# Attention, rotary mixing and a gated MLP in one kernel: first loads reordered, staging tiles borrowed, three mixing items and one weight conversion moved later

## The chip, the cores and the metric

One Trainium2 chip, of which the kernel uses one core. The metric is the device time of one execution in microseconds (us); lower is better. The kernel before takes 564.57 us, the median of 3 runs (564.46 to 564.57).

## The reference

Three blocks follow one another on 4 batches of 576 positions and 512 channels. The first is attention with 8 heads of 64 channels: heads 0 to 3 look at the last 32 positions, heads 4 to 7 at every fourth of the last 128. The second computes an angle and mixes:

```python
theta = x @ w_theta
zr, zi = x * cos(theta), x * sin(theta)
y = einsum('ts,bsd->btd', w_tok_r, zr) + einsum('ts,bsd->btd', w_tok_i, zi)
u = x + y
x = u + maximum(u @ w_ch, 0)
```

The third is a gated MLP:

```python
h = maximum(x @ w_in, 0);  u, v = h[..., :512], h[..., 512:]
v_s = einsum('ts,bsd->btd', w_spatial, layernorm(v)) + b_spatial
out = (u * v_s) @ w_out
```

The weights `w_theta`, `w_tok`, `w_ch`, `w_in` and `w_out` come as 64-bit floats.

## The kernel before, in words

All large products run on PE as three float32r products (high by high, low by high, high by low), so every weight and every activation is split into a high and a low part. A 64-bit weight chunk goes through `bits64` (L115): a DMA into a `w64` tile (4 buffers), one scaling on POOL or ACT into a `stage` tile (4 buffers), three bit operations on DVE through one PSUM tile `c64`; then `split_weight` (L136) makes the high part (`copy`, L107 to L111) and the low part (a subtraction, L144). Weights of the third block go back to DRAM by `stored` (L152): both parts in a `parts` tile (2 buffers), then a DMA into `win_d`, `wsp_d` or `wo_d`, from where they are loaded when there is room.

The order of the program, batch by batch:

- `attention(b)` (L300) makes 12 groups (4 head pairs by 3): scores on PE (L240; for batch 0 the mask is added on PE too, L233), softmax on DVE, ACT and POOL (L247 to L258), transposes (L268) two groups later, products with V (L282, L286) four groups later; ACT copies the result into `x` (L289 to L298). `att_load` (L196) issues the loads of K, Q and V, all on the SP queue; for batch 0 it is called for all four head pairs at once.
- `th_unit` (L326) makes the angle of 128 positions: `x` split on ACT or DVE (L339 to L342), 12 matmuls (L347), four transposes of `x` (L359), sine and cosine on ACT (L364, L365), and z split into `zh`, `zl` tiles. The last 64 positions of batches 2 and 3 share one unit, `th_shared` (L388), which starts from a copy `xs` (L332).
- `tm_run` (L402) mixes over positions: 8 items per batch, each 3 matmuls for each of 9 chunks of positions (L418, L425). For batch 2 the 8 items are made over 8 chunks first (24 matmuls each), and the ninth chunk, which waits for the shared unit, later.
- `ch_run` (L433) makes the product with `w_ch` (L444), 8 steps, and stores the result to `x2d`.
- The third block, for each batch: `hv_unit` (L617, five units, the fifth shared by two batches) with the normalisation on DVE, `hu_run` (L661), `sp_run` (L679), `out_unit` (L708).

`spread` (L458) interleaves one generator with others at given rates, so that attention of the next batch and weight conversions stand between mixing items. `second` (L490) is the list of conversions for the third block: 16 of `w_in`, 8 of `w_sp`, 8 of `w_out`. Twelve are taken in batch 1's stage, ten in batch 2's first stage (L520), and the rest while batch 3's angles are made (L521).

The program order is a priority, not the final order: when the kernel is built (L814, `schedule_with_timeline_sim=True`) a scheduler simulates the engines and gives each engine a fixed list, taking what it believes ready first. On the chip each engine then works its list in order, and a late input holds all that stands behind it. `tc.issue_after(ins)` forces what is traced inside it on the engine of `ins` behind `ins` in that list; it adds no wait.

PSUM has eight banks: `ps_mm` 4 (scores, angles, mixing, `w_ch`), `ps_t` 3 (transposes, V products), `ps_v` 1 (`c64`). After the second block the last two give way to `ps_2` with 4, which the third block uses alone.

```python
spread(tm_run(PAIR, K_MAIN, False), (chain(attention(PAIR + 1), th_shared(PAIR)), ATT_RATE_PAIR), (take(second, 10), 1.25))
spread(th_run(PAIR + 1, (0, 1, 2, 3)), (chain(tm_run(PAIR, (8,)), ch_run(PAIR)), TAIL_RATE), (second, 2.5))
```

Of the kernel before, what the change touches and what calls it, by code (L numbers as in the profile page):

```python
# [62 lines left out]
def tile_block(ctx: ExitStack, tc: tile.TileContext, qT, kT, vw, eye_in, mask_in, eye_b_in, w_theta, w_tok, w_ch, w_in, w_sp, w_sph, b_sp, w_out, out):  # L63
# [32 lines left out]
    wth_h = pth.tile([P, 4, DM], F32R, name="wth_h")  # L96
    wth_l = pth.tile([P, 4, DM], F32R, name="wth_l")
    patt = tc.alloc_tile_pool(name="patt", bufs=2, side="right")
    ps_t = tc.alloc_tile_pool(name="ps_t", bufs=3, space=PSUM)

    ps_v = tc.alloc_tile_pool(name="ps_v", bufs=1, space=PSUM)
    c64 = ps_v.tile([P, 512], F32, name="c64")


    def copy(dst, src, eng):
# [6 lines left out]

    last_dma = [None]

    def bits64(src, n, eng):  # L115

        p = src.shape[0]
        st = const.tile([P, 2 * CH], U32, tag="w64", name="w64", bufs=4)  # L120
        last_dma[0] = SY.dma_start(st[:p, :2 * n], src.bitcast(U32))
        w = st[:p, :2 * n].rearrange("p (n w) -> p n w", w=2)
        lw, hw = w[:, :, 0], w[:, :, 1]
        g = const.tile([P, CH], F32, tag="stage", name="w64g", bufs=4)[:p, :n]
        c = c64[:p, :n].bitcast(U32)
        gi = g.bitcast(U32)
        if eng == "a":
            A.mul(g, hw.bitcast(F32), 2.0**-112)
        else:
            G.tensor_scalar(g, hw.bitcast(F32), 2.0**-56, 2.0**-56, op0=ALU.mult, op1=ALU.mult)  # L130
        V.tensor_scalar(c, lw, 29, None, op0=ALU.logical_shift_right)
        V.scalar_tensor_tensor(c, gi, 3, c, op0=ALU.logical_shift_left, op1=ALU.bitwise_or)
        V.scalar_tensor_tensor(gi, gi, 0x80000000, c, op0=ALU.bitwise_and, op1=ALU.bitwise_or)
        return g

    def split_weight(src, hi, lo, eng_hi, eng_lo, eng_bits="g"):  # L136
        n = hi.shape[-1]
        if src.dtype == F32:
            s = const.tile([P, CH], F32, tag="stage", name="stage", bufs=4)[:src.shape[0], :n]
            SY.dma_start(s, src)  # L140
        else:
            s = bits64(src, n, eng_bits)
        copy(hi, s, eng_hi)
        (G if eng_lo == "g" else V).tensor_tensor(lo, s, f32(hi), op=ALU.subtract)  # L144

# [12 lines left out]

    def w_theta_job(k, c):
        cs = slice(DM // 2 * c, DM // 2 * (c + 1))  # L160
        split_weight(w_theta[:, k, cs], wth_h[:, k, cs], wth_l[:, k, cs], *THETA_ENG)

    def w_tok_job(k, c):
        cs = slice(CH * c, CH * (c + 1))
# [27 lines left out]
    groups = [(b, hp, g) for b in range(B) for hp in range(4) for g in range(3)]  # L192
    att = {}
    heads = {}

    def att_load(b, hp):  # L196
        early = b == 0 and hp >= 2
        qz = qz_2[hp - 2] if early else qzero[hp % 2]
        kt = kt_2[:, hp - 2] if early else patt.tile([P, S + WIN], F32, tag="k", name="kt", bufs=2)
        first = b == 0 and hp == 0  # L200
        n = KW + (NA - 1) * T
        for c0, c1 in ((0, n), (n, S + WIN)) if first else ((0, S + WIN),):
            SY.dma_start(kt[:, c0:c1], kT[b, hp, :, c0:c1])
            if c0 == 0:
                SY.dma_start(qz[:D, 0], qT[b, hp, :D])
            if first and c0 == 0:
                SY.dma_start(masks[:, :1], mask_in[:, :1])
                SY.dma_start(eye_b, eye_b_in)
        SY.dma_start(qz[D:, 1], qT[b, hp, D:])
        if first:  # L210
            SY.dma_start(masks[:, 1:], mask_in[:, 1:])
            SY.dma_start(ident, eye_in)
        vt = vt_2[:KW, hp - 2] if early else patt.tile([KW, NT, P], F32, tag="v", name="vt", bufs=2)
        SY.dma_start(vt, vw[b, hp])
        heads[b, hp] = (qz, kt, vt, {})
# [56 lines left out]
    def att_values(m):  # L272

        b, hp, g = groups[m]
        if g == 0:
            return
        qz, kt, vt, pT = heads[b, hp]
        ps = ps_t.tile([P, 512], F32, tag="pt", name="ps_x")
        if g == 1:
            for t in range(NA):  # L280
                for j in range(2):
                    PE.matmul(ps[T * j:T * (j + 1), T * t:T * (t + 1)], vt[:, t, T * j:T * (j + 1)], pT[j][:, T * t:T * (t + 1)], start=True, stop=True)  # L282
        else:
            for t in range(NB):
                for j in range(2):
                    PE.matmul(ps[T * j:T * (j + 1), T * t:T * (t + 1)], vt[:, NA + t, T * j:T * (j + 1)], pT[2][:, P * t + T * j:P * t + T * (j + 1)], start=True, stop=True)  # L286
        n0, n1 = (0, NA * T) if g == 1 else (NA * T, S)
        if hp < 2:
            A.copy(x[b][:, hp, n0:n1], ps[:, :n1 - n0])  # L289
            return  # L290

        xv = x[b][:, hp, :].rearrange("p (i r) -> p r i", r=4)
        if g == 1:
            A.copy(xv[:, :2, :], ps[:, :2 * SEQ].rearrange("p (r i) -> p r i", r=2))
            A.copy(xv[:, 2, :NA * T - 2 * SEQ], ps[:, 2 * SEQ:NA * T])
# [30 lines left out]
    def th_unit(b, t, pair=False):  # L326
# [29 lines left out]
        V.scalar_tensor_tensor(ta, ta, MAGIC, ps, op0=ALU.subtract, op1=ALU.subtract)  # L356
        xn = ps_t.tile([P, 512], F32, tag="pt", name="ps_xn")[:n]
        for k in range(4):
            PE.transpose(xn[:, P * k:P * (k + 1)], src[:, k, :], ident)  # L359
        if b == 0:  # L360
            A.activation(tb, ta, AF.Abs)
        else:
# [225 lines left out]

    for _ in ch_run(3):
        w3()  # L590
    p1.release()

    p2 = tc.alloc_tile_pool(name="p2", bufs=1, side="left", reuse_waits="tile")
    ps_2 = tc.alloc_tile_pool(name="ps_2", bufs=4, space=PSUM)

    wo_h = p2.tile([P, 4, DM], F32R, name="wo_h")
    wo_l = p2.tile([P, 4, DM], F32R, name="wo_l")
# [1 line left out]
        SY.dma_start(f32(t), f32(wo_d[:, :, i]))  # L599

    def mmtile(name):
        return ps_2.tile([P, 512], F32, tag="m2", name=name)

    vh, vl, vhl = {}, {}, {}
    hu = {}
# [126 lines left out]
    for pr in (0, 2):  # L732
# [85 lines left out]
```

## Time and profile before

| | us |
|---|---|
| median of 3 runs | 564.57 |
| the profiled execution | 564.04 |
| its span, first to last instruction | 562.2 |
| PE busy | 535.4 (95%) |
| DVE busy | 323.7 (58%) |
| POOL busy | 261.7 (47%) |
| ACT busy | 245.6 (44%) |

PE, DVE, ACT and POOL are the matrix, vector, scalar and GpSimd engines, SP issues DMAs (SPq is its queue), PEld is PE's weight load. "PEclk" is the granted clock of PE as a share of 2.4 GHz; 0.5 is 1.2 GHz. In a timeline row the bracket gives the idle time ahead of the instruction and what ended it. Busy is the union of an engine's instructions in a stretch. The durations of matmuls overlap, so their spacing, not their sum, is their cost.

### The profile page before, as it was taken

The page shows a single profiled execution, that of the slowest core. Times are in us where ns is not written, and L with a number is a line of the kernel's source. Part 1 is how long each engine was busy: PE and PEld are TensorE (multiplying, and loading weights), DVE is VectorE, ACT ScalarE, POOL GpSimd, SP SyncE. Part 2 cuts the span into 40 slices and gives each one's busy share as a digit, 9 for nine tenths or more (in the row PEclk, how much of TensorE's full clock was granted, in tenths as well). Part 3 has the DMA queues.
Part 4 walks back from the last instruction along what each step waited for, and adds up shares of the span by engine and source line. Part 5 has one row for each costly group of instructions (what it writes and reads, how often), then busy time and mean ns, then how long its engine had stood idle before and what let it go on. Part 6 is the DMA issues. An engine that isn't in the chain of part 4 may idle for free.

```text
span 562.2 us, 11265 instructions
## 1 busy us (share of the span) xinstructions
PE 535.4 (95%) x4148; PEld 477.2 (85%) x4148; DVE 323.7 (58%) x834; ACT 245.6 (44%) x718; POOL 261.7 (47%) x333
## 2 busy tenths in 40 slices
PE   4987999999999999996999999999999999999997
PEld 2765878888888988885979999899899889988996
DVE  2588998898887378656697116763701237353030
ACT  3768855525656444776354112432331224223222
POOL 3483995545975259744269334344201204322040
PEclk9899999999999999998899999999999999999999
DMA  7944956561468352785301999614015110002002
GB/s 188 234 139 126 238 152 194 178 188 62 144 200 236 109 180 96 239 244 170 116 1 43 325 362 355 208 35 136 11 64 168 39 56 1 1 1 76 1 0 94
DMA packets 50079, 76.07 MB, mean 135 GB/s; under 512 B 4068, under 2 KB 30824, under 8 KB 50024
## 3 DMA queue, kind: packets, MB, share of 16 engines
q1 hardware_dynamic: 50024, 75.35, 44.0%
q8 instruction: 33, 0.54, 0.4%
q14 instruction: 22, 0.18, 0.1%
HBM read 52.53 MB, written 22.81 MB: 134 GB/s over the span
## 4 chain that ended last, share of the span: by engine, by line
PE 63%; DVE 11%; DMA 8%; POOL 6%; ACT 5%; issue 5%; SPq 1%; POOLq 0%; DVEq 0%; ACTq 0%
PE ps_y L425 12%; PE ps_sp L693 9%; PE ps_hu L674 9%; PE ps_o L722 9%; PE ps_hv L629 9%; PE ps_r L444 5%; PE s L240 3%; DMA wsp_d<-parts 2%; PE pt L268 2%; DMA win_d<-parts 2%; POOL zl L319 2%; PE ps_x L282 2%; POOL parts L144 1%; DMA qz<-qT 1%; DMA x2d<-parts 1%
## 5 line engine op out<-in xcount | busy, mean ns | idle before, releaser
L425 PE MATMUL ps_y<-wtok_h,zh 128*128 128x288 f32 x270 | 82.7, 309 | 2.4 <-DVE sm L251 1.4
L425 PE MATMUL ps_y<-wtok_h,zl 128*128 128x288 f32 x270 | 81.3, 302 | 0.4 <-POOL zl L319 0.4
L425 PE MATMUL ps_y<-wtok_l,zh 128*128 128x288 f32 x270 | 80.3, 300 | 0.0
L319 POOL TENSOR_TENSOR gl<-hu,gh 128x288 fp32r<-128x288 f32 x32 | 26.0, 814 | 74.5 <-ACT gh L107 74.5
L425 PEld LDWEIGHTS ps_y<-wtok_h,zh 128*128 128x128 f32 x270 | 51.0, 190 | 5.9 <-DVE sm L251 2.1
L697 DVE TENSOR_TENSOR hu<-ps_sp,hu 128x288 f32<-128x288 f32 x32 | 14.6, 456 | 66.7 <-PE ps_sp L696 66.7
L425 PEld LDWEIGHTS ps_y<-wtok_h,zl 128*128 128x128 f32 x270 | 51.3, 190 | 1.9 <-POOL zl L319 0.8
L425 PEld LDWEIGHTS ps_y<-wtok_l,zh 128*128 128x128 f32 x270 | 51.0, 190 | 0.5
L319 POOL TENSOR_TENSOR vl<-hv,vh 128x512 fp32r<-128x512 f32 x16 | 20.9, 1308 | 62.6 <-ACT vh L107 55.2
L258 POOL TENSOR_TENSOR sm<-sm,l 128x288 f32<-128x288 f32 x48 | 32.6, 680 | 27.4 <-DVE l L257 22.1
L255 ACT ACTIVATE sm<-sm,m 128x96 f32<-128x96 f32 x108 | 39.2, 364 | 9.8 <-DVE m L252 7.5
L240 PE MATMUL s<-kt,qz 128*64 128x96 f32 x504 | 35.5, 268 | 4.6 <-DMA qz<-qT 3.4
L319 POOL TENSOR_TENSOR parts<-x,parts 128x288 fp32r<-128x288 f32 x32 | 26.6, 840 | 27.2 <-ACT parts L107 27.2
L693 PE MATMUL ps_sp<-wsp_h,vh 128*128 128x288 f32 x128 | 37.8, 295 | 0.0
L693 PE MATMUL ps_sp<-wsp_l,vh 128*128 128x288 f32 x128 | 37.8, 295 | 0.0
L693 PE MATMUL ps_sp<-wsp_h,vl 128*128 128x288 f32 x128 | 37.8, 295 | 0.0
L674 PE MATMUL ps_hu<-x2h,win_h 128*128 128x288 f32 x128 | 37.7, 294 | 0.0
L674 PE MATMUL ps_hu<-x2h,win_l 128*128 128x288 f32 x128 | 37.7, 294 | 0.0
L674 PE MATMUL ps_hu<-x2l,win_h 128*128 128x288 f32 x128 | 37.7, 294 | 0.0
L444 PE MATMUL ps_r<-uh,wch_l 128*128 128x288 f32 x128 | 37.7, 297 | 0.0
L444 PE MATMUL ps_r<-uh,wch_h 128*128 128x288 f32 x128 | 37.6, 298 | 0.0
L444 PE MATMUL ps_r<-ul,wch_h 128*128 128x288 f32 x128 | 37.4, 296 | 0.0
(180 smaller groups left out, 1570.0 us busy)
## 6 DMA issues: line engine op xcount, KB each, us to landing
x2d<-parts SPq DMA_DIRECT2D x32, 288.0 KB, 2.6
vt<-vw SPq DMA_DIRECT2D x16, 432.0 KB, 4.1
w<-w_tok SPq DMA_DIRECT2D x18, 288.0 KB, 3.0
x2h<-x2d SPq DMA_DIRECT2D x8, 576.0 KB, 7.4
x2l<-x2d SPq DMA_DIRECT2D x8, 576.0 KB, 10.7
kt<-kT SPq DMA_DIRECT2D x15, 304.0 KB, 5.3
w<-w_in SPq DMA_DIRECT2D x16, 256.0 KB, 3.5
win_d<-parts SPq DMA_DIRECT2D x16, 256.0 KB, 2.3
```

What stands on the lines that cost most here:

```text
L240: PE.matmul(o, qz[:, j, T * t:T * (t + 1)], kt[:, T * t:T * t + KW], start=not on_pe, stop=not on_pe)
L255: ia = A.activation(sm[:, t, :], src[:, t, :], AF.Exp, bias=m_[:, t:t + 1], scale=scale, accum_out=l[:, t:t + 1])
L258: ig = G.tensor_tensor(sm, sm, l.unsqueeze(2).to_broadcast([P, 3, KW]), op=ALU.mult)
L268: PE.transpose(pt[:KW, P * t:P * (t + 1)], sm[:, t, :], ident)
L319: return (G if el == "g" else V).tensor_tensor(dst_l, src, f32(dst_h), op=ALU.subtract)
L425: PE.matmul(ps[:, :CH], lh[b, k][:, P * d:P * (d + 1)], rh[:, k, cs], start=(n == 0), stop=(n == 3 * len(ks) - 1))
L444: PE.matmul(ps[:, :CH], lh[:, k, P * e:P * (e + 1)], rh[:, k, cs], start=(n == 0), stop=(n == 11))
L629: PE.matmul(ps, lh[:, k, ts_], rh[:, k, DM:], start=(n == 0), stop=(n == 11))
L674: PE.matmul(ps[:, :CH], lh[:, k, fs], rh[:, k, cs], start=(n == 0), stop=(n == 11))
L693: PE.matmul(ps[:, :CH], lh[b, k][:, fs], rh[:, k, cs], start=(n == 0), stop=False)
L697: V.tensor_tensor(t[:, f, cs], ps[:, :CH], t[:, f, cs], op=ALU.mult)
L722: PE.matmul(ps, lh[:, k, ts_], rh[:, k, cs], start=(n == 0), stop=(n == 11))
```

## The change

- `att_load`, batch 0: Q's first half and the small identity `eye_b` are issued from ACT's queue; the masks come in three pieces; V of a head pair is loaded one pair later, `ident` and the last masks with the second pair.
- `w_theta` is staged in the eight tiles `zh0..3`, `zl0..3`, which hold z later, and no longer in `w64`.
- Batch 2's mixing: five items are spread with attention of batch 3 and ten conversions; items six and seven are queued on PE behind the last V products of groups 46 and 47; then the shared unit and the first unit of batch 3; item eight is queued behind that unit's transposes.
- Two conversions (of `w_sp`) stay with batch 3's angles; the eight of `w_out` go, one per step, into `ch_run(3)`.
- `c64` is kept to the end; `ps_2` has 3 banks, and the third block alternates between `ps_2` and `ps_mm`.

```diff
-        split_weight(w_theta[:, k, cs], wth_h[:, k, cs], wth_l[:, k, cs], *THETA_ENG)
+        split_weight(w_theta[:, k, cs], wth_h[:, k, cs], wth_l[:, k, cs], *THETA_ENG, st=pz.tile([P, DM], U32, tag=f"z{'hl'[c]}{k}", name="wth64"))
...
-                SY.dma_start(qz[:D, 0], qT[b, hp, :D])
+                (A if first else SY).dma_start(qz[:D, 0], qT[b, hp, :D])
...
-                SY.dma_start(eye_b, eye_b_in)
+                A.dma_start(eye_b, eye_b_in)
...
-            SY.dma_start(masks[:, 1:], mask_in[:, 1:])
+            SY.dma_start(masks[:, 1:2], mask_in[:, 1:2])
...
+        if hp == 1:
             SY.dma_start(ident, eye_in)
+            SY.dma_start(masks[:, 2:], mask_in[:, 2:])
+        if hp:
+            SY.dma_start(heads[0, hp - 1][2], vw[0, hp - 1])
+        if hp == 3:
+            SY.dma_start(vt, vw[0, 3])
...
-    spread(tm_run(PAIR, K_MAIN, False), (chain(attention(PAIR + 1), th_shared(PAIR)), ATT_RATE_PAIR), (take(second, 10), 1.25))
-    spread(th_run(PAIR + 1, (0, 1, 2, 3)), (chain(tm_run(PAIR, (8,)), ch_run(PAIR)), TAIL_RATE), (second, 2.5))
+    tm = tm_run(PAIR, K_MAIN, False)
+    spread(take(tm, 7 - HELD), (attention(PAIR + 1), ATT_RATE_PAIR), (take(second, 10), 1.25))
+    for i in range(HELD):
+        with tc.issue_after(values[12 * (PAIR + 2) - HELD + i].ins):
+            next(tm)
+    run(th_shared(PAIR))
+    th = th_run(PAIR + 1, (0, 1, 2, 3))
+    next(th)
+
+    with tc.issue_after(turned[PAIR + 1, 0].ins):
+        run(tm)
+    spread(th, (chain(tm_run(PAIR, (8,)), ch_run(PAIR)), TAIL_RATE), (take(second, 2), 0.5))
...
     for _ in ch_run(3):
         w3()
+        next(second, None)
...
-    ps_2 = tc.alloc_tile_pool(name="ps_2", bufs=4, space=PSUM)
+    ps_2 = tc.alloc_tile_pool(name="ps_2", bufs=3, space=PSUM)
...
-        return ps_2.tile([P, 512], F32, tag="m2", name=name)
+        turn[0] += 1
+        return (ps_2 if turn[0] % 2 else ps_mm).tile([P, 512], F32, tag=("mm", "m2")[turn[0] % 2], name=name)
```

Here `HELD` is 2, `values[m]` is the last V product of group m and `turned[b, t]` the last transpose of a unit.

## Rows read from the trace of the kernel before

**Rows 1.** The page's busy time of PE, with share and number of instructions.
```profile
PE 535.4 (95%) x4148; PEld 477.2 (85%) x4148; DVE 323.7 (58%) x834; ACT 245.6 (44%) x718; POOL 261.7 (47%) x333
```
**Rows 2.** Busy time by stretch: start:end, length, then engines; granted clock, DMA share, GB/s.
```profile
4.75:13.00 8.25, 4.85 (x46) 3.02 (x46) 1.97 (x7) 3.73 (x21) 1.33 (x2) 0.91 0.95 224
24.70:45.00 20.30, 18.26 (x203) 12.89 (x199) 18.01 (x47) 13.77 (x53) 15.78 (x30) 1.00 0.51 145
45.00:84.30 39.30, 34.09 (x287) 28.55 (x287) 36.69 (x88) 31.61 (x85) 31.91 (x40) 1.00 0.64 174
84.30:224.00 139.70, 138.83 (x1234) 122.35 (x1233) 110.44 (x281) 70.58 (x215) 84.99 (x114) 1.00 0.54 160
224.00:258.40 34.40, 32.93 (x373) 28.54 (x371) 20.49 (x67) 24.27 (x99) 20.78 (x29) 1.00 0.73 222
258.40:265.30 6.90, 1.98 (x41) 1.54 (x40) 4.73 (x13) 4.53 (x15) 2.23 (x4) 0.91 0.63 188
265.30:272.30 7.00, 7.00 (x35) 6.90 (x36) 5.05 (x10) 1.69 (x5) 3.19 (x4) 0.60 0.54 171
272.30:295.50 23.20, 22.21 (x121) 18.77 (x119) 18.59 (x33) 11.29 (x20) 10.41 (x11) 1.00 0.10 30
343.00:376.50 33.50, 33.50 (x211) 31.00 (x210) 22.88 (x58) 13.38 (x32) 14.58 (x15) 1.00 0.51 174
```
**Rows 3.** PE's timeline at the start: start, us, instruction, idle before and its releaser.
```profile
4.75 0.42 PE L233 MATMUL s<-masks,eye_b 128*128 128x288 bf16 x1 [4.75 <-DMA eye_b<-eye_b]
...
12.98 1.23 PE L240 MATMUL s<-kt,qz 128*64 128x96 f32 x12 [3.40 <-DMA qz<-qT]
```
**Rows 4.** POOL's timeline: the first and the last operation on w_theta.
```profile
24.80 0.43 POOL L130 TENSOR_SCALAR w64g<-w 128x256 f32<-128x256 f32 x1 [0.47 <-DMA w<-w_theta]
...
42.07 0.73 POOL L144 TENSOR_TENSOR wth_l<-w64g,wth_h 128x256 fp32r<-128x256 f32 x1
```
**Rows 5.** SP's waits, 0 to 100 us: total, times, longest.
```profile
SPq L121 <- DVE c L131: 47.0, 24, 5.1
```
**Rows 6.** ACT's waits, 0 to 300 us: total, times, longest.
```profile
ACT parts L107 <- DMA wo_d<-parts: 6.4, 3, 3.5
...
ACT w64g L128 <- DMA w<-w_tok: 4.2, 3, 3.0
```
**Rows 7.** PE's timeline where attention of batch 3 ends.
```profile
259.25 0.50 PE L268 MATMUL pt<-ident,sm 128*96 128x128 f32 x3 [0.80 <-DVE pT L270]
...
261.92 0.57 PE L286 MATMUL ps_x<-pT,vt 96*64 96x64 f32 x12 [1.32 <-ACT pT L270]
265.29 1.09 PE L359 MATMUL ps_xn<-ident,xs 128*128 128x128 f32 x4 [2.80 <-DVE xs L332]
...
268.31 0.44 PE L425 MATMUL ps_y<-wtok_h,zh 128*128 128x288 f32 x1
```
**Rows 8.** ACT's and DVE's timeline in the same place.
```profile
263.34 0.40 ACT L107 CAST parts<-w64g 128x256 fp32r<-128x256 f32 x1 [0.53 <-DVE c L132]
263.65 0.66 ACT L294 COPY x<-ps_x 128x288 f32<-128x288 f32 x1
...
264.85 0.29 DVE L332 COPY xs<-x 128x256 f32<-128x256 f32 x1 [1.05 <-ACT x L298]
```
**Rows 9.** The chain that ended last, one mixing item of 27 matmuls.
```profile
108.11 3.60 PE ps_y L425 x27
```
**Rows 10.** DVE's timeline, first use of w_sp's last rows.
```profile
337.44 0.30 DVE L570 CAST wsp_hh<-stage 128x288 fp32r<-128x288 f32 x1
```
**Rows 11.** The shared normalised unit: DVE writes vhb, PE reads it.
```profile
375.63 0.42 DVE L658 CAST vhb<-hs 64x512 fp32r<-64x512 f32 x1
...
377.77 0.30 PE L696 MATMUL ps_sp<-wsp_lb,vhb 97*128 97x288 f32 x1
```
**Rows 12.** A DVE and a POOL operation side by side in the normalisation.
```profile
361.93 1.31 POOL L319 TENSOR_TENSOR vl<-hv,vh 128x512 fp32r<-128x512 f32 x1 [1.01 <-ACT vh L107]
362.19 1.07 DVE L642 TENSOR_TENSOR r<-r 128x1 f32<-128x1 f32 x1
```

More of the change, by code (lines that the diff above doesn't have):

```diff
@@ L49 @@
 PAIR = 2
+HELD = 2
 IN_ENG, SP_ENG, OUT_ENG = "vgg", "ag", "aga"
@@ L98, in tile_block @@
     patt = tc.alloc_tile_pool(name="patt", bufs=2, side="right")
-    ps_t = tc.alloc_tile_pool(name="ps_t", bufs=3, space=PSUM)
     ps_v = tc.alloc_tile_pool(name="ps_v", bufs=1, space=PSUM)
     c64 = ps_v.tile([P, 512], F32, name="c64")
+    ps_t = tc.alloc_tile_pool(name="ps_t", bufs=3, space=PSUM)
     def copy(dst, src, eng):
@@ L113, in tile_block, with bits64 @@
     last_dma = [None]
-    def bits64(src, n, eng):
+    def bits64(src, n, eng, st=None):
         p = src.shape[0]
-        st = const.tile([P, 2 * CH], U32, tag="w64", name="w64", bufs=4)
+        if st is None:
+            st = const.tile([P, 2 * CH], U32, tag="w64", name="w64", bufs=4)
         last_dma[0] = SY.dma_start(st[:p, :2 * n], src.bitcast(U32))
@@ L134, in bits64, with split_weight @@
         return g
-    def split_weight(src, hi, lo, eng_hi, eng_lo, eng_bits="g"):
+    def split_weight(src, hi, lo, eng_hi, eng_lo, eng_bits="g", st=None):
         n = hi.shape[-1]
@@ L141, in split_weight @@
         else:
-            s = bits64(src, n, eng_bits)
+            s = bits64(src, n, eng_bits, st)
         copy(hi, s, eng_hi)
@@ L194, in tile_block @@
     heads = {}
+    values = {}
     def att_load(b, hp):
@@ L204, in att_load @@
             if c0 == 0:
-                SY.dma_start(qz[:D, 0], qT[b, hp, :D])
+                (A if first else SY).dma_start(qz[:D, 0], qT[b, hp, :D])
             if first and c0 == 0:
                 SY.dma_start(masks[:, :1], mask_in[:, :1])
-                SY.dma_start(eye_b, eye_b_in)
+                A.dma_start(eye_b, eye_b_in)
         SY.dma_start(qz[D:, 1], qT[b, hp, D:])
         if first:
-            SY.dma_start(masks[:, 1:], mask_in[:, 1:])
-            SY.dma_start(ident, eye_in)
-        vt = vt_2[:KW, hp - 2] if early else patt.tile([KW, NT, P], F32, tag="v", name="vt", bufs=2)
-        SY.dma_start(vt, vw[b, hp])
-        heads[b, hp] = (qz, kt, vt, {})
+            SY.dma_start(masks[:, 1:2], mask_in[:, 1:2])
+        vt = vt_2[:KW, hp - 2] if early else patt.tile([KW, NT, P], F32, tag="v", name="vt", bufs=2)
+        heads[b, hp] = (qz, kt, vt, {})
+        if b:
+            SY.dma_start(vt, vw[b, hp])
+            return
+        if hp == 1:
+            SY.dma_start(ident, eye_in)
+            SY.dma_start(masks[:, 2:], mask_in[:, 2:])
[3 more added lines that the diff above has]
+            SY.dma_start(vt, vw[0, 3])
     def att_scores(m):
@@ L281, in att_values @@
                 for j in range(2):
-                    PE.matmul(ps[T * j:T * (j + 1), T * t:T * (t + 1)], vt[:, t, T * j:T * (j + 1)], pT[j][:, T * t:T * (t + 1)], start=True, stop=True)
+                    values[m] = PE.matmul(ps[T * j:T * (j + 1), T * t:T * (t + 1)], vt[:, t, T * j:T * (j + 1)], pT[j][:, T * t:T * (t + 1)], start=True, stop=True)
         else:
@@ L285, in att_values @@
                 for j in range(2):
-                    PE.matmul(ps[T * j:T * (j + 1), T * t:T * (t + 1)], vt[:, NA + t, T * j:T * (j + 1)], pT[2][:, P * t + T * j:P * t + T * (j + 1)], start=True, stop=True)
+                    values[m] = PE.matmul(ps[T * j:T * (j + 1), T * t:T * (t + 1)], vt[:, NA + t, T * j:T * (j + 1)], pT[2][:, P * t + T * j:P * t + T * (j + 1)], start=True, stop=True)
         n0, n1 = (0, NA * T) if g == 1 else (NA * T, S)
@@ L314, in tile_block @@
     zlast = {}
+    turned = {}
     uu = {}
@@ L358, in th_unit @@
         for k in range(4):
-            PE.transpose(xn[:, P * k:P * (k + 1)], src[:, k, :], ident)
+            turned[b, t] = PE.transpose(xn[:, P * k:P * (k + 1)], src[:, k, :], ident)
         if b == 0:
@@ L519, in tile_block @@
     th_keep(PAIR)
-    spread(tm_run(PAIR, K_MAIN, False), (chain(attention(PAIR + 1), th_shared(PAIR)), ATT_RATE_PAIR), (take(second, 10), 1.25))
-    spread(th_run(PAIR + 1, (0, 1, 2, 3)), (chain(tm_run(PAIR, (8,)), ch_run(PAIR)), TAIL_RATE), (second, 2.5))
+    tm = tm_run(PAIR, K_MAIN, False)
[9 more added lines that the diff above has]
+    spread(th, (chain(tm_run(PAIR, (8,)), ch_run(PAIR)), TAIL_RATE), (take(second, 2), 0.5))
     patt.release()
-    ps_v.release()
     ps_t.release()
@@ L590, in tile_block @@
         w3()
+        next(second, None)
     p1.release()
     p2 = tc.alloc_tile_pool(name="p2", bufs=1, side="left", reuse_waits="tile")
-    ps_2 = tc.alloc_tile_pool(name="ps_2", bufs=4, space=PSUM)
+    ps_2 = tc.alloc_tile_pool(name="ps_2", bufs=3, space=PSUM)
+    turn = [0]
     wo_h = p2.tile([P, 4, DM], F32R, name="wo_h")
@@ L755, in tile_block @@
     ps_2.release()
+    ps_v.release()
     p2.release()
```

## The prediction, made before the changed kernel ran

> **What bounds the kernel now.** I read the page's engine line first: PE is busy 535.4 of 562.2 us [rows 1], so 26.8 us without matmuls is nearly all there is to win, apart from the granted clock. The second view is the table of stretches, to see where those microseconds lie [rows 2]. From 84.3 to 224 us PE lacks 0.9 us of 139.7, and the stretch 343 to 376.5 has no gap: a faster side engine gives nothing there. The holes are in three places: the start (nothing until 4.75 us, then 3.40 of the next 8.25 us empty), the stage in which batch 0's angles are made (45 to 84.3 us: 5.2 us empty, with DVE busy 36.7 of 39.3), and the end of attention for batch 3 (258.4 to 265.3 us: 4.92 of 6.90 empty). Behind the last hole stands a second price: in the 7.00 us after it the granted clock is 0.60, that is mostly 1.2 GHz, with PE busy throughout; at 2.4 GHz that work would have taken 7.00 x 0.60 = 4.2 us, so 2.8 us are lost. The third view is the timeline at each hole, to see what ended it.
>
> **First loads.** Two waits stand at the start: the first matmul waits to 4.75 us for `eye_b`, and the first scores of head pair 1 wait 3.40 us for Q [rows 3]. All loads run in SP's order, and the DMA engines are 0.95 busy at 224 GB/s there [rows 2], so what counts is the bytes ahead. From the tile shapes (K 304 KB, Q 288, V 432, masks 4 x 72, `ident` 64, `eye_b` 32) pair 1's Q was behind 2000 KB and is now behind 1360: V of pair 0, `ident` and two masks moved back. 640 KB at 224 GB/s are 2.9 us, so the 3.40 us wait shrinks to some 0.5. `eye_b` goes from SP's fourth issue to ACT's second; I take 0.6 us (0 to 1.2; ACT has nothing else to do before the first scores are there). Attention of batch 0 is then 3.5 us ahead.
>
> Not all of that lives. Everything up to V of pair 3 is as many bytes as before, so the first chunk of `w_theta` can't come much before 24.80 us, when POOL starts on it; POOL ends the last at 42.07 + 0.73 = 42.8 [rows 4]. In those 18 us it does 8 chunks at 0.43 (L130) + as much for the high part, one input of the same size, + 0.73 = 1.6, so 12.7 us, and the softmax scalings still due, which are fewer by the lead. I let 2.5 of the 3.5 us live. Bounds: +1.0 (slower: V of pair 0 now lies behind 2000 KB instead of 1408, 592 KB or 2.7 us later, and the first V product may wait for it in PE's list) and -4.1 (2.9 + 1.2, all of it alive).
>
> **Staging `w_theta` in the z tiles.** SP waits 47.0 us in the first 100 for DVE to free a `w64` buffer, 24 times [rows 5]. With eight own tiles, `w_theta`'s loads wait for nothing, and four loads of `w_tok` can be under way before DVE reads any; ACT's waits for `w_tok`, 4.2 us in 3 [rows 6], go. What is late next is DVE: 36.7 of 39.3 us busy from 45 to 84.3 [rows 2], so no more than 2.6 us can be won there, and 2.3 (20.30 - 18.01) from 24.7 to 45. I take 1.5 us (0 to 4.9). The z tiles are first written after the chunks in them were read, since z needs the angle and the angle all of `w_theta`: no new wait.
>
> **Three items held back.** Before, two items of 24 matmuls stood behind the shared unit's transposes in PE's list and ran at 268.31, after the hole and mostly at the low clock, though they could have run in it [rows 7]. An item of 27 costs 3.60 us [rows 9], one of 24 then 3.2. Now one stands before the last V product (it covers the 1.32 us) and one behind it (it covers the 2.80 us from that product to `xs`); the 0.80 us ahead of them stays. The third stands behind the first unit's transposes and covers the split of `x`. So 4.1 us of holes go, and I let the clock's 2.8 us go with them, since PE then never rests there.
>
> The price is on the other side: one item that ran before 258.4 us is missing there. PE was busy 32.9 of 34.4 us in that stage, ACT 24.3, DVE 20.5 [rows 2]. If attention's chain follows PE, the stage ends 3.2 us sooner; if it goes at its own pace, 3.2 us become holes. I take 1.4. Sum for this part: -(4.1 + 2.8) + 1.4 = -5.5, between -10 (every hole from 224 to 295.5 us, 1.5 + 4.9 + 1.0, and the clock) and -0.9 (4.1 won, the 3.2 us come back whole and the clock stays).
>
> **`w_out` put off.** It is taken from the same place: the copy of `x` at 263.65 stands on ACT behind a cast for `w_out` that waited for DVE, and `xs` behind that copy [rows 8]; ACT waited 6.4 us there for `wo_d`'s stores [rows 6]. With the held items that chain is covered anyway, so I count it in the 1.4 above. Its new place is `ch_run(3)`. It needs `stage` tiles, and the four are with the last rows of `w_sp`, first read at 337.44 us [rows 10], so I expect it beside the first normalisations: 8 chunks of 1.3 us on DVE (three operations of this size at 0.43, as POOL's in [rows 4]), 0.8 on ACT (two at 0.40 [rows 8]), 0.73 on POOL. From 343 to 376.5 us these have 10.6, 20.1 and 18.9 us free [rows 2], but the normalisation's last write ends at 376.05, 1.7 us before PE needs it at 377.77 [rows 11]. I take 0 (0 to +12, worked out below). The parts themselves are wanted by `out_unit` alone, behind `hu_run`, `sp_run` and four units of the next batch.
>
> **PSUM.** Seven banks instead of four for the third block, in which PE had no gap: 0. `c64`'s longer life costs a bank that nothing wanted.
>
> **Sum.** -2.5 - 1.5 - 5.5 = -9.5. The profiled execution took 564.04 us (1.84 around the span), so 554.5; the median is 0.53 above that execution, so **555.1 us**.
>
> **Rivals.**
>
> *The hole only moves.* Attention of batch 3 keeps its own pace, the missing item leaves 3.2 us open, and the clock falls all the same. For it: DVE, ACT and POOL wait on one another there, none is full. Against it: PE was 96% busy. Then -2.5 - 1.5 - 4.1 + 3.2 = -4.9: 559.7 us.
>
> *The start is bound by conversion, not by loads.* DVE is 18.0 of 20.3 us busy from 24.7 to 45 and 36.7 of 39.3 after [rows 2]; the lead is waited away behind `w_theta`. Early gain 1.0 instead of 4.0: 558.1 us.
>
> *`w_out` holds the normalisation.* One DVE operation on a single number per partition took 1.07 us and ended at 363.26, with the POOL subtraction that began 0.26 us before it and ended at 363.24 [rows 12]: a POOL subtraction can hold DVE to its end. Eight more at 0.73 [rows 4] are 5.8 us; less 1.7 us of slack, PE waits 4.1 at the first `sp_run`: 559.2 us. The Trainium skill has this as a rule, in "SBUF — State Buffer", section "Who interferes with whom": a DVE instruction with two SBUF inputs and a GpSimd instruction that reads SBUF share a port pair, and the second to issue waits for the first in full. The pair in the trace agrees, with its 1.07 us.
>
> *Slower.* The mechanism is ACT's list in `ch_run(3)` and the units behind it: `w_out`'s casts write to two `parts` buffers, so six of eight wait for a store to DRAM, and the relu and the root of the normalisation stand behind them in order. At the old mean of 6.4 / 3 = 2.1 us [rows 6] that is 12.8 us, less 1.7 of slack 11.1, in which PE waits for the normalised tiles: 555.1 + 11.1 = 566.2 us. It decides against the change from 11.2 us of such waits, 1.9 each. Against it: the scheduler may place the casts late, and PE has the eight steps of `hu_run` in between.
>
> **How the numbers follow.** 0.50 for the forecast, whose own range is 551.5 to 558; 0.17 for the hole that moves, 0.13 for the conversion-bound start, 0.12 for the held normalisation, 0.08 for slower. From the first four about 0.05 falls within 0.2% (1.1 us, what a measurement of this kernel can tell from no change), so faster 0.87, same 0.05, slower 0.08. The best bounds together would go below 550; with 0.2 left out the range is 550.5 to 562.
>
> **What would show it.** Right: the first wait for Q near 0.5 us and the first matmul near 4; no waits of SP for DVE in `w_theta`'s loads; PE without a hole over 1 us between the last V products and the first angle of batch 3, at clock 1.00 there; mixing matmuls between V products of groups 46 and 47 and the transposes. Wrong: PE waits for `vt` near 13 us; holes of 3 us in 224 to 255; a PE wait at the first `ps_sp`, with ACT's `parts` casts waiting for `wo_d` ahead of it. The prediction fails as a whole if 84 to 224 us opens a hole, since it carries the early gain through.

## The result, and the profile after

The changed kernel takes 556.09 us, the median of 4 runs (554.9 to 556.45), against 564.52 for the kernel before beside it: a ratio of 0.9853, 95% interval [0.9837, 0.9869]. In a second session it came to 0.986 [0.9831, 0.989]. The prediction of 555.1 is 1.0 us off and the direction is right. The sum behind it is not: one of its terms was set at less than half of what it brought, one that stood at 0 was worth more than 5 us, and the two that were to bring 7 us together cost 2.8.

The profiled execution took 554.9 us. The busy line of its page, as [rows 1]:

```profile
PE 531.0 (96%) x4148; PEld 474.5 (86%) x4148; DVE 320.3 (58%) x835; ACT 244.2 (44%) x717; POOL 262.9 (48%) x333
```

The stretches that answer to [rows 2] (start:end, length, then PE, PEld, DVE, ACT, POOL busy; clock, DMA share, GB/s), cut at the same events, which now lie earlier:

```profile
5.80:13.00 7.20, 7.20 (x67) 4.54 (x69) 2.17 (x8) 3.77 (x21) 0.67 (x1) 1.00 0.94 234
...
24.20:45.00 20.80, 16.66 (x169) 11.74 (x168) 19.59 (x50) 14.50 (x45) 16.75 (x31) 1.00 0.47 154
45.00:81.00 36.00, 32.72 (x288) 27.72 (x287) 34.19 (x82) 27.62 (x78) 31.07 (x39) 1.00 0.64 175
81.00:216.00 135.00, 134.93 (x1205) 120.08 (x1201) 107.92 (x278) 69.78 (x212) 82.86 (x112) 1.00 0.55 163
216.00:253.50 37.50, 32.35 (x379) 27.42 (x377) 20.27 (x64) 23.80 (x98) 22.50 (x30) 1.00 0.66 200
253.50:257.00 3.50, 3.50 (x39) 3.11 (x40) 0.00 (x0) 1.32 (x3) 0.00 (x0) 0.58 0.00 0
257.00:266.00 9.00, 9.00 (x67) 8.32 (x64) 3.15 (x8) 0.58 (x3) 0.00 (x0) 0.97 0.01 2
...
334.00:367.00 33.00, 33.00 (x208) 30.55 (x207) 30.29 (x79) 18.21 (x45) 18.53 (x20) 1.00 0.73 241
```

The 3.40 us without PE in the first stretch are gone, and with them a low clock (0.91 and lower before). The end of attention for batch 3, from 257 us, has no hole. But the stage ahead of it now lacks 37.50 - 32.35 = 5.15 us of PE, where [rows 2] lacked 34.40 - 32.93 = 1.5 in the same place, and the low clock has moved to 253.5 us and become shorter. The third block has no gap, before or after. Measured at the first matmul of each stage, the changed kernel leads by 5.6 us when batch 2's mixing begins (212.7 against 218.2), by 9.1 when the third block begins, and by 9.1 at the end.

PE's timeline at the start and in that stage (start, us, instruction, idle before it and its releaser; lines are those of the changed kernel, up to 13 higher than before):

```profile
5.80 0.42 PE L245 MATMUL s<-masks,eye_b 128*128 128x288 bf16 x1 [5.80 <-DMA eye_b<-eye_b]
...
242.06 0.50 PE L280 MATMUL pt<-ident,sm 128*96 128x128 f32 x3 [1.69 <-ACT x L301]
...
251.57 0.53 PE L280 MATMUL pt<-ident,sm 128*96 128x128 f32 x3 [1.83 <-POOL sm L270]
253.00 0.53 PE L280 MATMUL pt<-ident,sm 128*96 128x128 f32 x3 [0.90 <-POOL sm L270]
...
256.31 0.44 PE L438 MATMUL ps_y<-wtok_h,zl 128*128 128x288 f32 x1
256.68 0.91 PE L298 MATMUL ps_x<-pT,vt 96*64 96x64 f32 x12
257.52 0.40 PE L438 MATMUL ps_y<-wtok_l,zh 128*128 128x288 f32 x1
```

The last three rows are the held items at work: mixing stands on both sides of the last V product. The three rows above them are what [rows 7] did not have at this size. ACT's and POOL's rows at two of these holes say who was late:

```profile
241.10 0.43 ACT L108 CAST parts<-stage 128x288 fp32r<-128x288 f32 x1 [1.94 <-issue]
241.44 0.47 ACT L301 COPY x<-ps_x 128x384 f32<-128x384 f32 x1
```

```profile
250.09 0.81 POOL L146 TENSOR_TENSOR parts<-stage,parts 128x288 fp32r<-128x288 f32 x1 [1.84 <-ACT parts L108]
250.84 0.67 POOL L270 TENSOR_TENSOR sm<-sm,l 128x288 f32<-128x288 f32 x1
```

In both an instruction of attention stands in its engine's list right behind one of a `w_sp` conversion, ahead of which the engine had stood idle for 1.94 and 1.84 us. The copy could have run when ACT fell idle, at 239.16: the V products that it reads (L294) had ended at 238.05.

### The profile page after: what moved, and what is told of

It is laid out like the page before. It is cut to its first block, busy times and chain, and to the rows that moved or that the text cites. A ratio compares the mean times of both kernels' runs of the same rounds, so it can differ in the third digit from the quotient of the medians.

```text
span 553.1 us, 11234 instructions
## 1 busy us (share of the span) xinstructions
PE 531.0 (96%) x4148; PEld 474.5 (86%) x4148; DVE 320.3 (58%) x835; ACT 244.2 (44%) x717; POOL 262.9 (48%) x333
## 4 chain that ended last, share of the span: by engine, by line
PE 52%; DMA 3%; POOL 1%; ACT 1%; issue 1%; DVE 1%; SPq 0%; ACTq 0%; POOLq 0%; DVEq 0%
PE ps_sp L719 9%; PE ps_hu L700 9%; PE ps_o L748 9%; PE ps_hv L655 9%; PE ps_y L438 7%; PE ps_r L457 4%; PE ps_th L360 1%; DMA wsp_d<-parts 1%; DMA win_d<-parts 1%; PE ps_sp L722 1%; PE ps_sp L721 1%; POOL zl L332 0%; POOL parts L146 0%; ACT parts L108 0%; DVE ta L381 0%
## 5 line engine op out<-in xcount | busy, mean ns | idle before, releaser
L267 ACT ACTIVATE sm<-sm,m 128x96 f32<-128x96 f32 x108 | 39.2, 364 | 12.8 <-DVE m L264 6.7
L332 POOL TENSOR_TENSOR ul<-x,uh 128x288 fp32r<-128x288 f32 x32 | 26.7, 841 | 26.4 <-ACT uh L108 26.1
L441 DVE TENSOR_TENSOR x<-ps_y,x 128x288 f32<-128x288 f32 x40 | 17.6, 448 | 33.9 <-PE ps_y L438 33.8
```

Source lines behind the costliest of these rows:

```text
L267: ia = A.activation(sm[:, t, :], src[:, t, :], AF.Exp, bias=m_[:, t:t + 1], scale=scale, accum_out=l[:, t:t + 1])
L332: return (G if el == "g" else V).tensor_tensor(dst_l, src, f32(dst_h), op=ALU.subtract)
```

## The experiments

Twelve kernels ran. Each edit is given against the changed kernel or the kernel before. Ratios are against the kernel before, run in the same session (its medians: 562.9, 565.38 and 564.62). The four kernels named u_ with one part undone share the first session, o_held and the l_ kernels the third; the changed kernel ran in the second (after_again), so against it the others are compared by their ratios. The expectations of the first session were reckoned from 564.52, and the kernel before took 1.6 us less there, so that a time in us flatters these four.

| kernel | what it has of the change | median us | ratio, interval |
|---|---|---|---|
| u_loads | all but the first loads | 560.68 | 0.9955 [0.9934, 0.9977] |
| u_stage | all but the staging | 556.73 | 0.9884 [0.9841, 0.9927] |
| u_held | all but the held items | 555.88 | 0.9885 [0.9846, 0.9923] |
| u_wout | all but w_out's move | 557.69 | 0.99 [0.9857, 0.9942] |
| after_again | all | 556.42 | 0.986 [0.9831, 0.989] |
| o_wout | w_out's move alone | 559.52 | 0.9907 [0.9886, 0.9927] |
| u_stage_held | loads and w_out | 553.64 | 0.9795 [0.977, 0.982] |
| f_nocast | all; ten conversions later | 553.51 | 0.9795 [0.9767, 0.9822] |
| l_nohold | loads, w_out; twelve conversions behind attention | 557.53 | 0.9872 [0.9852, 0.9892] |
| l_nohold_stage | the same, and staging | 556.28 | 0.9859 [0.9837, 0.988] |
| l_hold | as l_nohold, and held items | 552.76 | 0.9782 [0.9763, 0.9802] |
| o_held | held items alone | 562.48 | 0.9967 [0.9949, 0.9986] |

For the stage of batch 3's attention and angles, this is what the profiled executions show: its length from batch 2's first mixing matmul to its first `ps_r`, PE's idle time up to the last V product and behind it, and the mean clock of these two parts.

| kernel | length | idle, up to V | idle, behind | clock |
|---|---|---|---|---|
| before | 77.2 | 4.0 | 3.8 | 1.00, 0.90 |
| o_held | 74.4 | 4.5 | 0.6 | 0.93, 1.00 |
| u_loads | 72.7 | 3.5 | 0.3 | 0.92, 1.00 |
| o_wout | 72.4 | 3.7 | 2.2 | 1.00, 1.00 |
| u_wout | 75.4 | 5.6 | 0.6 | 0.93, 1.00 |
| u_stage | 72.4 | 4.5 | 0.3 | 0.96, 1.00 |
| u_held | 73.3 | 3.7 | 2.2 | 0.96, 1.00 |
| after, after_again | 73.2, 72.1 | 5.2, 4.1 | 0.3 | 0.96, 1.00 |
| u_stage_held | 71.3 | 3.0 | 2.2 | 1.00, 1.00 |
| f_nocast | 70.9 | 2.9 | 0.3 | 0.96, 1.00 |
| l_nohold | 74.2 | 0.6 | 4.3 | 1.00, 0.90 |
| l_nohold_stage | 74.4 | 0.4 | 6.3 | 1.00, 0.95 |
| l_hold | 68.1 | 0.5 | 1.1 | 1.00, 1.00 |

**u_loads.** `att_load` is that of the kernel before.

```diff
-                (A if first else SY).dma_start(qz[:D, 0], qT[b, hp, :D])
+                SY.dma_start(qz[:D, 0], qT[b, hp, :D])
...
-            SY.dma_start(masks[:, 1:2], mask_in[:, 1:2])
+            SY.dma_start(masks[:, 1:], mask_in[:, 1:])
+            SY.dma_start(ident, eye_in)
...
```

> The changed kernel with its first loads put back (all on SP, masks and ident in one piece, V of each pair with its K and Q); staging, held items and w_out as changed. Theory (the early lead of 5.5 us comes mostly from the byte order and the clock that no longer falls behind the Q hole): first matmul back near 4.75, the 3.4-us wait for Q and a stretch at 1.2 GHz behind it are back, the first ps_y of batch 2 near 216.5, time 559.5 to 560.5. Rival (the lead of the loads is waited away behind w_theta, and staging makes the gain): first ps_y of batch 2 by 213.5, time 556 to 557.5.

Measured 560.68, a ratio of 0.9955 where the theory's 559.5 to 560.5 are 0.991 to 0.993 of 564.52: the loads bring rather more than it had. Against the changed kernel 0.9955 - 0.986 is 0.95%, 5.4 us, by the two intervals 3 to 7. The wait for Q is back, and the low clock around it (PE's timeline, then a stretch):

```profile
11.78 1.16 PE L243 MATMUL s<-kt,qz 128*64 128x96 f32 x12 [2.05 <-DMA qz<-qT]
```

```profile
10.00:16.00 6.00, 4.22 (x42) 3.06 (x42) 1.51 (x6) 3.07 (x18) 1.33 (x2) 0.72 1.04 259
```

From 10 to 18.5 us all four kernels with the old loads have a clock of 0.60 to 0.80, and all ten profiles with the new loads 1.00 (four of these have 0.66 to 0.70 later, from 26 to 36 us). Yet the start is not the greater part. In the profiled executions the 51st mixing matmul stands 1.8 us later than in the changed kernel (67.80 against 65.97), the 433rd, batch 2's first, 4.0 us later (216.72 against 212.68). From the 51st to the 217th mixing matmul (batch 0's mixing to batch 1's) the four old-load kernels take 73.1 to 73.2 us and the new-load ones 72.1 to 72.6, at clock 1.00 and with nearly the same idle time, 1.2 to 1.6 us. PE's fixed list differs there: counted in the traces, neighbours in it are of two kinds (mixing, scores, V products and so on) 90 times with the old loads and 71 times with the new, in every kernel of either sort. From the 217th to the 433rd it is 61 times and 57, and without their idle time the stretches take 75.4 us with the old loads and 74.5 to 75.0 with the new. Rows of u_loads show what such a place looks like:

```profile
85.45 0.27 PE L285 MATMUL ps_x<-pT,vt 96*64 96x64 f32 x1
85.47 0.30 PE L243 MATMUL s<-kt,qz 128*64 128x96 f32 x1
85.56 0.22 PE L285 MATMUL ps_x<-pT,vt 96*64 96x64 f32 x1
85.60 0.27 PE L243 MATMUL s<-kt,qz 128*64 128x96 f32 x2
```

So the load order, an edit of the first microseconds, gave the scheduler other times to plan with, and it wrote another list for stages that follow 50 us later. That the smaller number of switches is the 1.0 us there fits but was not isolated.

**u_stage.** `w_theta` goes through `w64` again.

```diff
-        split_weight(..., *THETA_ENG, st=pz.tile([P, DM], U32, tag=f"z{'hl'[c]}{k}", name="wth64"))
+        split_weight(..., *THETA_ENG)
```

> The changed kernel with w_theta staged in w64 again. Theory (staging is worth what I forecast): +1.5 us, 557.6, with SP waiting for DVE in w_theta's loads. Rival (staging makes the early gain): +4 us, 560. Second rival (w_tok's loads wait for DVE in either case, 44.0 us against 47.0): within 0.5 us of 556.1.

Measured 556.73, a ratio of 0.9884; the interval does not tell this from the changed kernel, and 1.5 us is not excluded. But the trace shows that the wait only changed its owner. SP's waits in the first 100 us (total, times, longest), of the changed kernel and of this one:

```profile
SPq L123 <- DVE c L133: 44.0, 18, 12.4
```

```profile
SPq L123 <- DVE c L133: 47.8, 26, 4.7
```

18 waits for 26, with the same total: `w_theta` is loaded by 24 us, and SP then stands 12.4 us at once in front of `w_tok`, while the DMA engines have a share of 0.01 from 32 to 40 us (0.62 without staging). DVE, which frees the `w64` tiles, is near full in both: 15.06 us of 16 from 24 to 40 us in the changed kernel, 14.84 here.

**u_held.** All eight mixing items stand with attention again, by the old `spread` line.

```diff
-    spread(take(tm, 7 - HELD), (attention(PAIR + 1), ATT_RATE_PAIR), (take(second, 10), 1.25))
...
-        run(tm)
+    spread(tm_run(PAIR, K_MAIN, False), (chain(attention(PAIR + 1), th_shared(PAIR)), ATT_RATE_PAIR), (take(second, 10), 1.25))
```

> The changed kernel with nothing held back: all eight mixing items of batch 2 are spread with attention of batch 3, the shared unit follows it, as before; w_out stays in ch_run(3), two conversions stay with the angles. Theory (the held items close the holes and spare clock, at a price of their own): a hole of 2.5 to 3 us at the shared unit's transposes and about 7 us at 1.2 GHz are back, holes ahead of it shrink from 5.2 to 4 us: 559.5. Rival (taking w_out's casts from there closes the hole by itself): hole under 1 us, time 555.5 to 556.5.

Measured 555.88, in us the rival's time; but the ratio of 0.9885 lies between the rival's (0.984 to 0.986 of 564.52) and the theory's (0.991), and its interval holds both. The time does not decide, the trace does: without any held item the 2.80-us hole of [rows 7] is 1.34 (not under 1, as the rival had it), and the clock is 1.00 behind it. The idle time in front of it fell by about what came back behind it (5.2 and 0.3 in the changed kernel; here 3.7 and 2.2). Of these 3.7 us 2.73 are one hole, behind ACT's copy of `x` and a cast of `w_sp` ahead of that copy, as in the changed kernel (PE's timeline, then the two parts of the stage):

```profile
244.59 0.85 PE L280 MATMUL pt<-ident,sm 128*96 128x128 f32 x3 [2.73 <-ACT x L301]
```

```profile
214.10:258.60 44.50, 40.83 (x468) 35.47 (x468) 24.97 (x70) 26.64 (x105) 26.41 (x34) 0.96 0.61 185
258.60:287.40 28.80, 26.57 (x162) 23.23 (x158) 19.98 (x37) 11.95 (x23) 9.59 (x10) 1.00 0.00 1
```

**u_wout.** `w_out`'s conversions stand beside batch 3's angles as before.

```diff
-    spread(th, (...), (take(second, 2), 0.5))
+    spread(th, (...), (second, 2.5))
...
-        next(second, None)
```

> The changed kernel with the eight conversions of w_out back beside batch 3's angles and none in ch_run(3). Theory (the held items cover that chain, and in ch_run(3) w_out costs nothing): 556 to 557. Rival (w_out's casts and stores hold the chain of x, and moving them made the gain of 3.6 us of that stage): 559 to 560. Rival on the other side (w_out in ch_run(3) costs something that no PE hole shows): 554.5 to 555.5.

Measured 557.69, between theory and rival (its ratio of 0.99 is 558.9 of 564.52, close to the rival), and its interval overlaps that of the changed kernel. The stage is 2.2 to 3.3 us longer, with 0.93 for 0.96 of clock. This called for w_out alone.

**after_again.** The changed kernel, unedited.

> The changed kernel itself once more, as the base for the kernels beside it. Every theory: 0.985 of the kernel before, executions spread over some 2 us because the stretches at 1.2 GHz fall in other places from one execution to the next.

Six executions took 554.92 to 559.3; the three at a mean clock of 0.997 took 554.9 to 555.5, those at 0.985 to 0.988 took 557.4 to 559.3. A comparison of single executions of two versions can be off by 3 us in this way. The mean clock does not tell all of it: l_nohold took 557.1 us at 1.000 and 556.72 at 0.984.

**o_wout.** The kernel before, with `next(second, None)` in `ch_run(3)`, `(take(second, 2), 0.5)` beside the angles, and PSUM grouped as changed.

> The kernel before with one part of the change alone: w_out's eight conversions go to ch_run(3), two conversions stay with batch 3's angles (and PSUM is grouped as changed, which that needs). Theory (taking w_out's casts out of ACT's list is what closes the hole at the shared unit's transposes): the 2.80-us hole shrinks to under 1 us, the stretch from batch 2's first mixing to its first ps_r goes from 77.3 to about 73.5 us, 3.5 to 4 us faster than before. Rival (my prediction: w_out's old place cost at most what the held items cover): 0 to 1.5 us faster, the hole stays over 2 us.

0.9907, that is 5.3 us (4.1 to 6.4): more than the theory's 3.5 to 4, and nearly four times the 1.4 that the prediction counted it in. What remains of the hole, and the stretch behind it, of which [rows 2] show 0.60 of clock (PE's timeline, then the stretch):

```profile
265.34 0.63 PE L363 MATMUL ps_xn<-ident,xs 128*128 128x128 f32 x4 [1.34 <-DVE xs L336]
```

```profile
263.80:292.60 28.80, 26.55 (x160) 23.20 (x156) 20.03 (x37) 11.94 (x23) 9.65 (x10) 1.00 0.00 1
```

2.80 us became 1.34, and in this stage the clock did not fall at all. From batch 3's first `ps_r` to the end both kernels take 225.3 us, so the new grouping of PSUM has no part in the gain. In [rows 8] a cast for `w_out` holds the copy of `x`; it is not there any more.

**u_stage_held.** The edits of u_stage and u_held together.

> The changed kernel without the staging and without the held items: only the first loads and w_out's move are left. Theory (these two are the whole gain): within 0.8 us of the changed kernel beside it. Rival (staging 1.5 and held items at least 3, as I forecast): 4 to 5 us slower than the changed kernel.

553.64: 2.8 us faster than the changed kernel beside it, and the intervals of the two do not touch. The profiled execution is its slowest, 554.83, so that trace understates it. Its stage has clock 1.00 in both parts, and the largest hole in it is 1.34 us. That loads and w_out are the whole gain holds, with more than that: the rest of the change costs 2.8 us. From o_wout to this kernel the medians differ by 5.9 us, the ratios by 1.12%, 6.3 us; that is what the first loads bring.

**f_nocast.** The ten conversions beside attention come with the angles.

```diff
-    spread(take(tm, 7 - HELD), (attention(PAIR + 1), ATT_RATE_PAIR), (take(second, 10), 1.25))
+    spread(take(tm, 7 - HELD), (attention(PAIR + 1), ATT_RATE_PAIR))
...
-    spread(th, (...), (take(second, 2), 0.5))
+    spread(th, (...), (take(second, 12), 3.0))
```

> The changed kernel with none of the ten conversions beside attention of batch 3; they stand with the other two beside batch 3's angles. Theory (casts and subtractions of w_in and w_sp in ACT's and POOL's lists hold attention's chain there): PE's idle time from batch 2's first mixing to the last V product falls from 5.2 to under 2.5 us; if they find room later, 2 to 3 us faster than the changed kernel. Rival (attention's own chain of DVE, ACT and POOL sets the holes): idle stays at 4.5 to 5.5 us, time within 1 us. On the other side: the conversions hold batch 3's angles (DVE is 18.6 of 23.2 us busy there) or the first loads of w_in come late: 1 to 4 us slower.

553.51, 2.9 us faster than the changed kernel; the two holes behind POOL are gone, the idle time up to V is 2.9 (2.5 was the bound). The hole behind ACT's copy of `x` stayed at 1.88, since the scheduler still put two casts ahead of that copy: a later place in the program is no later place in the list. And a new wait appeared in the third block (PE's, POOL's and DVE's timelines):

```profile
367.46 0.40 PE L721 MATMUL ps_sp<-wsp_hh,vhl 128*128 128x288 f32 x1 [1.09 <-POOL vhl L683]
```

```profile
364.35 1.65 POOL L146 TENSOR_TENSOR parts<-w64g,parts 128x256 fp32r<-128x256 f32 x2
366.08 2.77 POOL L683 TENSOR_TENSOR vhl<-hv,hs 64x512 fp32r<-64x512 f32 x2
```

```profile
366.21 1.48 DVE L684 CAST vhb<-hs 64x512 fp32r<-64x512 f32 x1
```

Two subtractions for `w_out` stand in POOL's list ahead of the shared normalised unit. In the changed kernel POOL starts on that unit at 364.04, with nothing ahead of it.

**l_nohold.** The kernel of u_stage_held, with twelve conversions put behind attention in the lists of ACT, DVE and POOL by `issue_after` (behind the last copy of `x`, `values[47, 0]`, and the last softmax).

```diff
-    spread(tm_run(...), (chain(...), ATT_RATE_PAIR), (take(second, 10), 1.25))
+    spread(tm_run(...), (chain(...), ATT_RATE_PAIR))
...
-    spread(th, (...), (take(second, 2), 0.5))
+    spread(th, (...), (jobs([lambda: behind((values[47, 0],) + softmax[47][1:], lambda: next(second))] * 12), 3.0))
```

> First loads and w_out's move alone, and the twelve conversions that remain are queued on ACT, DVE and POOL behind attention of batch 3 (the last copy of x and the last softmax), beside batch 3's angles. Theory (conversions standing in ACT's and POOL's lists hold attention's chain): PE's idle time from batch 2's first mixing to the last V product falls under 1.5 us (2.97 with the conversions among them), no stretch at 1.2 GHz there, 0.975 to 0.978 of the kernel before. Rival (attention's own chain, or the conversions cost as much behind it): 0.979 to 0.983.

The mechanism holds and the forecast fails. Idle time up to V is 0.6 us, so conversions in the engines' lists were what held attention of batch 3; the edit moves them on ACT, DVE and POOL together and does not tell which list held most. But the time is 0.9872, worse than 0.9795: the conversions now hold the angles. Two stretches (the profiled execution is the slowest of the six), then PE's, ACT's and DVE's timelines:

```profile
216.80:256.90 40.10, 39.48 (x468) 34.55 (x468) 25.50 (x75) 24.51 (x97) 19.62 (x27) 1.00 0.36 107
256.90:290.90 34.00, 29.70 (x160) 25.77 (x156) 23.55 (x44) 15.00 (x31) 18.36 (x20) 0.90 0.49 148
```

```profile
276.01 0.40 PE L438 MATMUL ps_y<-wtok_h,zh 128*128 128x288 f32 x1 [2.12 <-ACT zh L108]
```

```profile
270.90 0.43 ACT L108 CAST parts<-stage 128x288 fp32r<-128x288 f32 x1 [1.94 <-DMA wsp_d<-parts]
271.36 1.28 ACT L377 ACT_TABLE_LOAD   x1
272.65 0.63 ACT L377 ACTIVATE ta<-ta 128x512 f32<-128x512 f32 x1
273.19 0.71 ACT L378 ACTIVATE tb<-tb,half_pi 128x512 f32<-128x512 f32 x1
...
275.34 0.62 ACT L108 CAST zh<-zz 128x512 fp32r<-128x512 f32 x1 [0.25 <-DVE zz L389]
```

```profile
273.93 0.68 DVE L388 TENSOR_TENSOR zz<-ps_xn,tb 64x512 f32<-64x512 f32 x1 [2.30 <-ACT tb L378]
```

PE waits for `zh`, `zh` for DVE's z, and that 2.30 us for the sine on ACT. In ACT's list the sine and the load of its table stand behind a cast that had waited 1.94 us for the store of its `parts` buffer.

**l_nohold_stage.** The same with the staging of the change.

> The kernel beside it (loads, w_out, conversions behind attention) with w_theta staged in the z tiles as changed: the one difference is the staging. My prediction: 1.5 us faster than without. Theory now (SP waits for DVE in w_tok's loads in its stead, and the DMA engines stand idle from 32 to 40 us): 0 to 2 us slower than without, the first ps_y of batch 2 no earlier.

0.9859 against 0.9872, intervals that overlap. It neither shows the forecast 1.5 us nor excludes it; a cost of more than 1 us, as the theory allowed, is not there. The hole in front of `zh` is there again, 4.21 us long in this profile.

**l_hold.** The same as l_nohold with the three items held back.

> The same (loads, w_out, conversions behind attention, no staging) with the three items held back as changed: the one difference from the first kernel is the holding. Theory (the held items cover 1.9 us at the shared unit, and open as much in attention by their absence): within 0.8 us of the kernel without holding. My prediction's: 4 us faster or more. Rival: with attention's chain free of conversions nothing opens there, 1 to 2 us faster.

0.9782: 0.9%, some 5 us, faster than l_nohold; here my theory fails and the prediction's 4 us and more are right. Two stretches as above:

```profile
214.20:252.70 38.50, 38.04 (x452) 32.75 (x452) 24.48 (x73) 25.18 (x98) 19.43 (x27) 1.00 0.34 99
252.70:282.30 29.60, 28.46 (x175) 25.11 (x171) 23.70 (x47) 13.65 (x26) 15.36 (x18) 1.00 0.49 151
```

With the conversions out of attention's way the three items leave no hole where they are missing (0.5 us), and fill those that l_nohold has behind V (1.1 for 4.3). This is the fastest kernel of the study, about 4 us ahead of the changed one. It pays 0.92 us at the same place of the third block as f_nocast.

**o_held.** The kernel before with the held items of the change alone.

> The kernel before with one part alone: the three items held back as changed, w_out where it was. My prediction: 5.5 us faster. Theory now (holding and w_out's move close the same hole; this one costs a hole elsewhere, and the clock falls behind that): 1 to 2.5 us faster. On the other side, that the missing item and the casts of w_out in ACT's list cost more than the hole: 0 to 2 us slower.

0.9967 [0.9949, 0.9986], 1.9 us, as the theory had it. The hole behind V closes, holes of 1.71, 0.89 and 1.50 us open in attention, and the clock falls there.

## Why the prediction was right, and where it was not

**First loads, -2.5: mis-sized.** They bring 5.4 us (u_loads) to 5.9 or 6.3 (o_wout to u_stage_held, by medians or ratios). The wait for Q went altogether, where 0.5 us was to stay. The first matmul did not come earlier: 5.80 us, not "near 4". ACT issues `eye_b` sooner than SP did (1.32 against 2.42 us), but it landed later (ACT's queue in the changed kernel):

```profile
0.73 0.55 ACTq L208 DMA_DIRECT2D qz<-qT  x1
1.32 0.60 ACTq L211 DMA_DIRECT2D eye_b<-eye_b  x1
1.95 1.28 ACT L260 ACT_TABLE_LOAD   x1 [1.95 <-issue]
```

In the ten profiles with the new loads the first matmul stands at 4.80 to 5.92, eight of them over 5.5, and at 4.56 to 4.75 in the four with the old ones: this part of the step costs some 1 us. Why `eye_b` lands late was not tried. What the step left out is the clock behind the Q hole (0.91 in [rows 2], 0.54 from 11 to 18.5 us when one asks for that stretch), and that a new load order gives a new list. The prediction said that 84 to 224 us "carries the early gain through"; it added to it.

**Staging, -1.5: not found.** No run shows a gain or a cost of it by itself. What was expected in the trace, `w_theta`'s loads without a wait, is there. What is late next is DVE, as the step said, and at once: it is busy 15.06 us of 16 from 24 to 40 us, and the next user of the four `w64` tiles, `w_tok`, waits for it. No gain can be seen of the 2.3 and 2.6 us of DVE's idle time that the step took as its bounds.

**Held items, -5.5: the failing step.** It took the hole at the shared unit for want of filler. The sentence that failed is the one under w_out: "With the held items that chain is covered anyway, so I count it in the 1.4 above." [Rows 8] had the cause in them, a cast for `w_out` ahead of the copy of `x`. Taking that cast away brings 5.3 us by itself, in the hole (2.80 to 1.34) and in the clock behind it; the held items alone bring 1.9. Both close the same hole, so their sum is not 7.2: with w_out gone, u_held shows nothing clear of noise left for the held items. The missing item's price, taken as 1.4 between 0 and 3.2, was 0.4 to 1.5 us of holes (4.1 and 5.2 in the two profiles of the changed kernel, less 3.7 in u_held). Behind such holes, in o_held, the changed kernel and u_wout, the clock falls too.

**w_out put off, 0: right for its new place, wrong for its old one.** No wait at the first `ps_sp` and no gap in the third block. The rival "w_out holds the normalisation" did not happen, but it is near: in f_nocast and l_hold PE waits 1.09 and 0.92 us there, not 4.1, and it is by POOL's list: in f_nocast POOL takes up the unit 0.70 us after DVE does (366.08, 365.38). The prediction's mechanism can be seen on DVE too: its first cast of `vhl`, 0.41 us in the changed kernel (at 364.02), takes 0.90 in f_nocast (at 365.38) beside the second subtraction for `w_out`. The cast of `vhb`, 0.42 us alone in [rows 11], takes 1.48 beside POOL's subtraction of the same unit, which has nothing to do with `w_out`: it is 1.51 in the changed kernel and, for the other batch of the unit, in the kernel before. The Trainium skill states in "SBUF — State Buffer", section "Who interferes with whom", that casts on DVE can take the port pair shared with GpSimd and that the later one then waits in full; the stretched casts agree. PE waited for POOL's part of `vhl`, and for none of these casts. The slower rival, stores holding ACT's list in `ch_run(3)`, is there at a third of its size: ACT waits 4.8 us in 3 for `wo_d`'s stores (12.8 were reckoned), and PE has no gap.

**Why the total came out.** Measured along one path, by the medians of one session: w_out -5.9, first loads -5.9, staging and held items together +2.8, in sum -9.0 (by the ratios -5.3, -6.3 and +3.7, in sum -7.9); forecast were 0, -2.5 and -7.0, in sum -9.5. Three errors of 3 to 10 us cancelled; that the total came within 1.0 us is luck. The rival of a hole that only moves had the sign of the held items right, for holes opened in attention and the clock fell behind them. Its reason, that attention keeps its own pace, does not hold: with the conversions out of its way PE idles 0.5 us there (l_hold). Open is how the 2.8 us divide: with staging or held items undone singly the time does not change measurably, with both undone it falls. The stage table puts 0.8 to 1.9 us of it on that stage, its holes and its clock. Where the rest lies is not shown: the profile of u_stage_held is of its slowest execution and comes to batch 2's mixing later than the changed kernel (214.91 us against 212.68 and 213.98), with a clock of 0.70 from 26 to 36 us.

## What to carry to other kernels

When a hole's releaser is an engine that is far from full, look at the instruction ahead of the late one in that engine's list before looking for filler: a conversion that itself waits holds all that stands behind it, and removing it beat covering it by 5.3 us to 1.9. Two edits that close the same hole must not be summed, and each is best run alone on the kernel before: filler was worth 1.9 us here on the kernel before, nothing measurable with `w_out` gone, and 5 us with the other conversions out of attention's way too. Where a scheduler writes the lists, count every edit as a new list for all later stages.

## What was not expected of the hardware

The clock's price at a hole depends on its size in no simple way: behind 2.80 us the row shows 0.60 for 7.00 us, behind 1.83 and 0.90 it shows 0.58 for 3.50, behind 4.21 in l_nohold_stage 0.57 for 4.00 and then 1.00, and in o_wout, with holes of 1.52, 1.21 and 1.34, it stays at 1.00. It also differs between executions of the same kernel, whose mean clock ran from 0.985 to 0.997 and whose time from 554.92 to 559.3 us.
